# 120 further TensorE products of 128 to 512 columns behind the last product of a windowed-attention and gated-convolution kernel

## The chip, the cores and the metric

The kernel runs on one core of one Trainium2 chip. The metric is device time in microseconds of one execution. Times of the profile are microseconds from the start of the span, which goes from the first to the last instruction of the program on the core.

## The reference

Inputs are q, k and v of shape (8, 8, 576, 64) (batch, heads, positions, head width), a matrix w_in of 512 x 1024, three rows conv_w of 1024, and a matrix w_out of 1024 x 512. A causal attention with a window of 64 positions is followed by a layer with a gate, whose gate comes from a convolution along the positions:

```
scores = scale * np.matmul(q, k.transpose(0, 1, 3, 2))
mask = (rel >= 0) & (rel < window)
scores = np.where(mask, scores, -1000000000.0)
attn = np.exp(scores - max) / (sum + 1e-09)
x = np.matmul(attn, v)              # heads side by side: (8, 576, 512)
h = np.maximum(x @ w_in, 0.0)
conv_out[s] = sum over k of conv_w[k] * h[s + k - 1]
out = h * (1 / (1 + np.exp(-conv_out))) @ w_out
```

(The lines are shortened; the row maximum and the row sum are those of the softmax.)

## The kernel before, in words

The 8 x 576 = 4608 positions are cut into 12 units of 384 columns (`NU`, `NX`). For each unit the kernel makes the scores of six 64-wide blocks per head (`qk`, L371), the masked row maximum on VectorE (`row_max`, L378), the exponentials on ScalarE (`exps`, L388), the normalised rows (`normalise`, L399), their transposes (`transpose_pe`, L404, for the first two units; by VectorE and small transfers for the others), and the product with v (`values`, L522). The attention's result is split into a high and a low part, `xh` and `xl`, so that products in the rounded float32 kind give nearly full precision: each product of the layer is three, high times high, low times high and high times low. `mm1` (L542) multiplies by w_in, whose parts lie in `wih` and `wil`: per unit 8 slices of 128 hidden columns times 4 slices of the inner dimension times 3, each product with 128x128 weights and 384 columns. Then come the relu (L565), the convolution (`conv_mid` L571, `conv_side` L578), the sigmoid (L585), the gate (L590) and its split into `gh` and `gl` (L594, L598). `mm2` (L607) multiplies by w_out (`woh`, `wol`): again 8 x 4 x 3 products a unit, of 384 or 386 columns.

The eight PSUM banks of 512 columns are two `sc` (scores), two `acc` (`values` and `mm1` take turns) and four `po` (`mm2`, one per 128 output columns). At the end of a unit `po` is copied into `ot` by ScalarE (L647) and VectorE (L649), which lies in a tile named `T`, and SyncE issues a transfer to DRAM. In the last unit there is one transfer for each of the first three output slices (L651); the fourth is copied and sent in two halves (L643, L644).

The order of the work is a plan: every piece of work is a `Work` with a due time, an engine and a cost, `queued` simulates the engines with these costs and gives one list, and the last two lines of `attention_moe` issue the list in that order. Between pieces of the first 110 us it also puts products of a tile `spare` (`keep_busy`, L219: 112 columns, always the same 128x128 weights), whose results nobody reads. The program's closing part has the line number of the launch call, L778 (L783 in the changed kernel): each engine drains, SyncE waits for its transfers, and the engines meet at semaphores before they end. The program's opening part has L771.

Of the kernel before, what the change touches and what calls it, by code (L numbers as in the profile page):

```python
# [174 lines left out]
def attention_moe(ctx: ExitStack, tc: tile.TileContext, q, k, v, w_in, conv_w, w_out, out):  # L175
# [533 lines left out]
    with tc.manual_schedule():  # L709
        for x in queued(plan, keep_busy):  # L710
            x.do()


_INS = ['q', 'k', 'v', 'w_in', 'conv_w', 'w_out']

# [66 lines left out]
```

## Time and profile before

| | us |
|---|---|
| median of two runs | 518.82 |
| the two runs | 517.61, 520.02 |
| span of the profiled execution | 514.3 |
| TensorE busy in that span | 504.4 |
| last product of TensorE starts | 509.75 |

The profile is of one execution; for that execution it states its span alone. In a row of the timeline the first number is the start and the second the length of a merged group of instructions, then come engine, line, operation, output and inputs, the weights' size, the shape and the count. PE is the product on TensorE, PEld the load of its weights; a trailing q (SPq, PEldq) is the engine's own sequencer, which issues transfers and handles semaphores. A row of a line's view has min/median/max of the duration in ns and then the first and the last start in us. In the rows of windows the last three numbers are the granted TensorE clock, the busy share of the DMA engines and the GB/s.

### The profile page before, as it was taken

To read this page: it belongs to the slowest core of one execution; us is meant where nothing else is said; L and a number is where in the kernel's file an instruction comes from. 1 tells how busy PE (TensorE), PEld (TensorE's weight loads), DVE (VectorE), ACT (ScalarE), POOL (GpSimd) and SP (SyncE) were. 2 spreads that over 40 slices of the span, in tenths; PEclk is the share of its full clock that TensorE was granted. 3 is DMA by queue.
4 is the path that set the end of the run, shared out by engine and by line. 5 is a ranking of instruction groups with operands and counts; after the bars stand their busy time and mean duration, and the time that the engine had idled before them with its cause. 6 is when DMAs were issued, how large, how long until landed. Compare 5 with 4: busy or idle time off the path is not lost.

```text
span 514.3 us, 14601 instructions
## 1 busy us (share of the span) xinstructions
PE 504.4 (98%) x5710; PEld 487.0 (95%) x5710; DVE 367.0 (71%) x1088; ACT 380.0 (74%) x1013; POOL 91.2 (18%) x188
## 2 busy tenths in 40 slices
PE   8989998999999999999999999999999999999996
PEld 8878997999999999999999999999999999999996
DVE  4999998987855767666686967666766766645870
ACT  5989998889577888597687696786877866534640
POOL 7113332212020131020220221212202102000000
PEclk9999999999999999999999999999999999999999
DMA  8984963538225244444344343442541321100111
GB/s 302 357 318 142 322 213 111 175 83 324 74 63 176 82 141 144 124 142 148 112 154 149 104 141 115 146 146 71 187 157 46 106 67 46 62 1 0 63 63 62
DMA packets 29461, 69.96 MB, mean 136 GB/s; under 512 B 5712, under 2 KB 17616, under 8 KB 29392
## 3 DMA queue, kind: packets, MB, share of 16 engines
q1 hardware_dynamic: 29392, 69.03, 40.3%
q8 instruction: 45, 0.74, 0.6%
q14 instruction: 24, 0.20, 0.1%
HBM read 47.73 MB, written 9.47 MB: 111 GB/s over the span
## 4 chain that ended last, share of the span: by engine, by line
PE 89%; DVE 5%; ACT 2%; DMA 2%; issue 0%; SPq 0%; DVEq 0%; ACTq 0%
PE po L607 40%; PE acc L542 36%; PE acc L522 6%; PE sc L371 5%; DVE s L378 2%; PE acc L219 1%; DMA bits<-in_w_out_dram 1%; DVE T L262 1%; ACT T L256 1%; DMA q<-in_q_dram 1%; PE po L371 1%; DVE wil L280 1%; DVE s L399 1%; ACT ub L409 0%; DVE xl L529 0%
## 5 line engine op out<-in xcount | busy, mean ns | idle before, releaser
L607 PE MATMUL po<-gh,woh 128*128 128x386 f32 (+1 forms) x384 | 132.7, 346 | 0.0
L607 PE MATMUL po<-gh,wol 128*128 128x386 f32 (+1 forms) x384 | 130.0, 339 | 0.0
L542 PE MATMUL acc<-xh,wih 128*128 128x384 f32 x384 | 129.8, 338 | 0.1
L607 PE MATMUL po<-gl,woh 128*128 128x386 f32 (+1 forms) x384 | 129.7, 338 | 0.0
L542 PE MATMUL acc<-xh,wil 128*128 128x384 f32 x384 | 128.8, 335 | 0.0
L542 PE MATMUL acc<-xl,wih 128*128 128x384 f32 x384 | 128.7, 335 | 0.0
L578 DVE SCALAR_TENSOR_TENSOR c<-hbuf,cw,c 128x386 f32<-128x386 f32 (+1 forms) x192 | 111.6, 634 | 16.3 <-ACT c L571 16.1
L388 ACT ACTIVATE s<-s,nm 128x96 f32<-128x96 f32 (+2 forms) x288 | 105.1, 369 | 3.0 <-DVE nm L378 2.8
L399 POOL TENSOR_TENSOR s<-s,r 128x768 f32<-128x768 f32 x27 | 41.8, 1547 | 231.0 <-DVE r L394 180.4
L607 PEld LDWEIGHTS po<-gh,woh 128*128 128x128 f32 x384 | 72.2, 188 | 2.5
L542 PEld LDWEIGHTS acc<-xh,wih 128*128 128x128 f32 x384 | 72.2, 188 | 0.7 <-ACT hbuf L565 0.2
L607 PEld LDWEIGHTS po<-gl,woh 128*128 128x128 f32 x384 | 72.4, 189 | 0.0
L607 PEld LDWEIGHTS po<-gh,wol 128*128 128x128 f32 x384 | 72.3, 188 | 0.0
L542 PEld LDWEIGHTS acc<-xh,wil 128*128 128x128 f32 x384 | 72.2, 188 | 0.0
L542 PEld LDWEIGHTS acc<-xl,wih 128*128 128x128 f32 x384 | 72.1, 188 | 0.0
L571 ACT ACTIVATE c<-hbuf,cw 128x386 f32<-128x386 f32 (+1 forms) x96 | 53.6, 609 | 18.4 <-DVE gl L598 18.3
L598 DVE TENSOR_TENSOR gl<-c,gh 128x772 fp32r<-128x772 f32 (+1 forms) x48 | 47.3, 986 | 22.8 <-ACT gh L594 21.9
L590 DVE TENSOR_TENSOR c<-c,hbuf 128x772 f32<-128x772 f32 (+1 forms) x48 | 46.3, 972 | 19.9 <-ACT c L585 19.7
L378 DVE CUSTOM_DVE_ANT_0 s<-sc,mask 128x96 f32<-128x96 f32 (+2 forms) x260 | 49.1, 254 | 16.0 <-PE sc L371 15.5
L594 ACT CAST gh<-c 128x772 fp32r<-128x772 f32 (+1 forms) x48 | 40.1, 836 | 24.1 <-PE po L607 15.5
L388 ACT ACTIVATION_READ_ACCUMULATOR s<-s,nm 128x1 f32 x288 | 55.0, 191 | 0.0
L565 ACT ACTIVATE hbuf<-acc 128x384 f32<-128x384 f32 x64 | 30.9, 484 | 28.3 <-PE acc L542 28.3
(63 smaller groups left out, 561.1 us busy)
## 6 DMA issues: line engine op xcount, KB each, us to landing
v<-in_v_dram SPq DMA_DIRECT2D x24, 768.0 KB, 5.8
ub<-T SPq DMA_DIRECT2D x240, 48.0 KB, 1.9
k<-in_k_dram SPq DMA_DIRECT2D x22, 448.0 KB, 4.1
q<-in_q_dram SPq DMA_DIRECT2D x22, 384.0 KB, 5.6
out_dram<-T SPq DMA_DIRECT2D x8, 772.0 KB, 3.7
bits<-in_w_in_dram SPq DMA_DIRECT2D x8, 512.0 KB, 8.7
bits<-in_w_out_dram SPq DMA_DIRECT2D x8, 512.0 KB, 5.7
out_dram<-T SPq DMA_DIRECT2D x3, 768.0 KB, 4.8
```

The lines of the kernel that those rows point to most:

```text
L371: nc.tensor.matmul(bank_of(u, b, i, h)[r:r + rows, o:n], qs[hs, 2 * g + p, t:t + rows], ks[hs, 2 * g + p, t + o:t + n], start=True, stop=True)
L378: nc.vector.tensor_tensor_reduce(out=ss[b][:, i, h, o:n], in0=bank_of(u, b, i, h)[:, o:n], in1=mask[m][:, o:n], scale=-0.125, scalar=3.0e3 ...
L388: nc.scalar.activation(x, x, AF.Exp, bias=nms[b][:, e], scale=-1.0, accum_out=sms[b][:, e])
L399: on.tensor_tensor(sv, sv, rs[b][:, e].unsqueeze(2).broadcast_to([P, e.stop - e.start, n]), ALU.mult)
L542: nc.tensor.matmul(acc[bank(("m", u, f))][:, :NX], w[:, f, c], x[u % 2][:, c], start=(c == 0 and j == 0), stop=(c == NC - 1 and j == 2))
L565: nc.scalar.activation(hbuf[:, f, o:o + NX], ps[:, :NX], AF.Relu)
L571: nc.scalar.activation(cs[i % 2][:, a, :n], hbufs[u % 2][:, f, 1:1 + n], AF.Copy, scale=cw[:, 1, f:f + 1])
L578: nc.vector.scalar_tensor_tensor(c, hbufs[u % 2][:, f, e:e + n], cw[:, e, f:f + 1], c, op0=ALU.mult, op1=ALU.add)
L590: nc.vector.tensor_tensor(c, c, hbufs[u % 2][:, 2 * i:2 * i + 2, 1:1 + n], ALU.mult)
L594: nc.scalar.copy(ghs[ring(u, i)][:, :, :n], cs[i % 2][:, :, :n])
L598: nc.vector.tensor_tensor(gls[ring(u, i)][:, :, :n], cs[i % 2][:, :, :n], ghs[ring(u, i)][:, :, :n].bitcast(F32), ALU.subtract)
L607: nc.tensor.matmul(po[o][:, :n], w[:, f, es], x, start=(f == 0 and j == 0), stop=(f == NF - 1 and j == 2))
```

## The change

Behind the loop that issues the plan, still in the same program, ten groups of twelve products are issued on TensorE. Group g writes the first n columns of `acc[g % 2]`, each product with its own start and stop. The moving operand is always the first n columns of `xh[1]`, read across its four slices (4 x 384 columns lie side by side). The weights are the 128x128 blocks of `wih`, block number `i // reuse`: a new block for each product where `reuse` is 1, the same block for all twelve where it is 12, a new block for every second where it is 2. Nothing reads these results.

```
     for x in queued(plan, keep_busy):
         x.do()
 
+    flat_x, flat_w = xh[1].rearrange("p c n -> p (c n)"), wih.rearrange("p f c e -> p (f c) e")
+    for g, (n, reuse) in enumerate(((512, 1), (512, 12), (448, 1), (416, 1), (384, 1), (384, 12), (384, 2), (256, 1), (128, 1), (128, 12))):
+        for i in range(12):
+            nc.tensor.matmul(acc[g % 2][:, :n], flat_w[:, i // reuse], flat_x[:, :n], start=True, stop=True)
```

On TensorE the listings of the two programs differ in the last rows; `acc_107` and `acc_108` are the two `acc` banks, `xh_64` is `xh[1]`, and the shape is partitions x columns.

```order
@@ -1,3 +1,3 @@
-L778 UNCONDITIONAL_BRANCH
+L783 UNCONDITIONAL_BRANCH
 L219 MATMUL acc_107<-spare 128x112 x9
 L371 MATMUL sc_105<-k,q 64x64
@@ -3429,3 +3429,13 @@
 L607 MATMUL po_112<-gh_97,wol 128x386
 L607 MATMUL po_112<-gl_100,woh 128x386
-L778 UNCONDITIONAL_BRANCH
+L716 MATMUL acc_107<-xh_64,wih 128x512 x12
+L716 MATMUL acc_108<-xh_64,wih 128x512 x12
...
+L716 MATMUL acc_107<-xh_64,wih 128x128 x12
+L716 MATMUL acc_108<-xh_64,wih 128x128 x12
+L783 UNCONDITIONAL_BRANCH
```

All rows ahead of these, on TensorE and on the other engines, are the same in both programs but for the line numbers of the launch; the new products stand between the last L607 product and the closing part.

## The prediction

> **What bounds the kernel now.** I read the page first: its busy shares, its clock digits and its chain.
>
> ```profile
> span 514.3 us, 14601 instructions
> PE 504.4 (98%) x5710; PEld 487.0 (95%) x5710; DVE 367.0 (71%) x1088; ACT 380.0 (74%) x1013; POOL 91.2 (18%) x188
> PEclk9999999999999999999999999999999999999999
> PE 89%; DVE 5%; ACT 2%; DMA 2%; issue 0%; SPq 0%; DVEq 0%; ACTq 0%
> ```
>
> TensorE is busy for 98% of the span, holds 89% of the chain that ended last, and has its clock granted all the way. Work added to it in the middle would cost its full length. This work is added at the end, so what matters is what else still runs when TensorE is done. Next I read the chain of waits near its end and the timeline of the last two microseconds.
>
> ```profile
> 471.94 38.16 PE po L607 x216
> 510.10 0.02 issue
> 510.12 0.37 DVE T L643
> 510.49 0.02 issue
> 510.52 0.32 ACT T L643
> ...
> 509.75 0.34 PE L607 MATMUL po<-gl,woh 128*128 128x386 f32 x1
> 510.59 0.90 SPq L644 DMA_DIRECT2D out_dram<-T  x2
> ```
>
> The last 216 products of L607 run without a gap, 38.16 / 216 = 0.177 us each, and the last ends at 509.75 + 0.34 = 510.09. Two half copies by VectorE and ScalarE follow, then two transfers to DRAM, the second of which is issued by 511.5. The span ends at 514.3, so 4.2 us pass after the last product. The view of the end-of-program line L778, SyncE's waits there and the landing time of the last transfers tell what fills them.
>
> ```profile
> L778 SPq EVENT_SEMAPHORE  x7: 17/27/28, 513.0 to 514.2; - x7
> L778 POOLq EVENT_SEMAPHORE  x4: 17/17/17, 513.6 to 514.2; - x4
> L778 SPq DRAIN  x3: 7/7/7, 513.6 to 513.9; - x3
> L778 PEldq DRAIN  x2: 13/1695/3377, 506.8 to 513.9; - x2
> ...
> SPq L778 <- DMA out_dram<-T: 1.8, 2, 1.5
> ...
> L644 SPq DMA_DIRECT2D out_dram<-T x2: 402/406/409, 510.6 to 511.1; - x2
> ...
> DMA to landing us min/median/max: 2.2/2.3/2.4
> ```
>
> TensorE's sequencer reaches its drain at 506.8 and stands in it for 3.38 us, to about 510.15: it is finished 0.05 us after its last product. SyncE waits for the last transfer (issued at about 511.1, 2.2 us to landing, so 513.3), and the engines meet at 513.6, where GpSimd's first semaphore row stands. From that meeting to the end of the span it is 514.3 - 513.6 = 0.7 us. **TensorE therefore has 513.6 - 510.15 = 3.45 us of cover**: so much added work is free, and every microsecond beyond it moves the meeting and the end by one.
>
> **The change, part by part.** It removes nothing and moves nothing. It adds 120 products on TensorE behind the last L607 product: 24 of 512 columns, 12 of 448, 12 of 416, 36 of 384, 12 of 256 and 24 of 128, together 12288 + 5376 + 4992 + 13824 + 3072 + 3072 = 42624 columns. Their operands (xh, wih) were written long before, the banks (acc) were last read long before, and the listing of the changed program has no wait on them, so I let the first start right behind the last L607 product and the rest follow without a gap. No transfer, no copy and no other engine's instruction is added. The copies and transfers of the tail read other banks and buffers than these products write; were one late, it would have the added length itself as cover.
>
> The price of one product is its start-to-start time, not its record, since the records overlap. The nearest rows are those of L542: same weights, same kind of data, 384 columns, in a stretch where TensorE waits for nothing.
>
> ```profile
> L542 PE MATMUL acc<-xh,wil x31: 334/334/337, 61.1 to 76.7; 128*128 128x384 f32 x31
> L542 PEld LDWEIGHTS acc<-xl,wih x31: 187/188/188, 61.1 to 76.7; 128*128 128x128 f32 x31
> ...
> 16.01 1.39 PE L404 MATMUL po<-ident,s 128*128 128x128 f32 x11
> ...
> L404 PE MATMUL po<-ident,s x11: 272/273/295, 16.0 to 17.1; 128*128 128x128 f32 x11
> ...
> L219 PE MATMUL acc<-spare 128*128 128x112 f32 x74 | 12.2, 332 | 1.0 <-DVE spare L222 1.0
> L219 PEld LDWEIGHTS acc<-spare 128*128 128x128 f32 x74 | 11.3, 240 | 1.7 <-DVE spare L222 1.0 <-issue 0.7
> ```
>
> Of three interleaved groups, one has 31 products from 61.1 to 76.7, so 30 steps of three: 15.6 / 90 = 0.1733 us for 384 columns, 0.4514 ns a column. L607 with 386 columns took 0.177. The narrow end has only plain float32 rows: the 128-column transposes of L404 start (1.39 - 0.27) / 10 = 0.112 us apart, when the last record of 0.27 us is taken off.
>
> Widths other than these two have no row, so each is bounded from both sides:
> - By columns alone (all of the 173.3 ns streams): 512 columns 231.1 ns, 448 202.2, 416 187.8, 384 173.3, 256 115.6, 128 57.8. The sum is 42624 x 0.4514 = 19.24 us.
> - By a line through the two rows (0.24 ns a column and a fixed part of 81): 204, 189, 181, 173, 143 and 112 ns. The sum is 24 x 204 + 12 x 189 + 12 x 181 + 36 x 173.3 + 12 x 143 + 24 x 112 = 19.98 us.
> - By columns, but no product under 112 ns: 19.24 + 24 x (112 - 57.8) / 1000 = 20.54 us.
> - No product under the 173.3 of a 384-column one, if the weight load (a record of 188 ns, longer than the spacing) set that spacing: 19.24 + 24 x 0.1155 + 12 x 0.0577 = 22.7 us.
>
> These ends are close together, because wide products lose in the second reading what narrow ones gain. I take the first, 19.24, and raise it by 0.1, some 3 ns on each of the 36 narrow ones, since the 4 ns between L542 and L607 are not two columns: **19.35 us**. The rows of L542 are of the very operands used here. L404 and L219 work on other data (float32 instead of the rounded kind), and L219 has 18 records between 1 and 5 us for 9 calls in the program, so that kind is issued in another way than the products of L542, which are one to a call.
>
> [...]
>
> Repeated weights: in 36 products all twelve of a group have the same weights, and 12 more have each twice. I price them like the others. The L219 rows are that case: every product has the same 128x128 tile as its weights, and there are as many weight loads as products (x74 and x74). If the repeated load (11 + 11 + 11 + 6 = 39 of them) were nevertheless left out, the first reading, in which a load has no price, saves nothing; the second saves at most its fixed part, 39 x 0.081 = 3.2 us, so 16.8 us in all and a time of 532.2.
>
> The sum: TensorE's last product ends at 510.09 + 19.35 = 529.44, its drain 0.05 later, the end 0.7 later, at 530.2. Against 514.3 that is **+15.9 us** (19.35 - 3.45). The page gives no time of the profiled execution but its span of 514.3; the two timed runs lie 3.3 and 5.7 us above that, their median 518.82 lies 4.5 above. What lies around the span is launch and end, which the change does not touch, so I add to the median: 518.82 + 15.9 = **534.7 us**.
>
> **The rivals.**
>
> *Narrow products have a floor (slower than forecast).* The 128-column products cost 112 ns or more each, because a weight load cannot be finished sooner. For it: L404's spacing, and load records of 188 ns beside a spacing of 173. Against it: those rows are float32. With the 20.54 us of above the time is 518.82 + 17.1 = 535.9; with 22.7 it is 538.1.
>
> *More than two products in flight (not slower by over 2%).* A record of L542 lasts 334 ns and the next starts after 173, so about two are under way at once. Those products add up in one bank in a chain of twelve; the added ones stand alone, each with its own start and end. If that chain is what holds the spacing, three could be under way: 334 / 3 = 111 ns for 384 columns, 42624 x 0.290 = 12.4 us, +8.9, so 527.7. It decides if the spacing falls below (10.4 + 3.45) / 42624 = 0.325 ns a column, 10.4 us being 2% of 518.82. Against it: L607 changes bank after every three products and gains nothing by it (0.177). [...]
>
> *The change does not do what it says (same).* Products that nobody reads could be dropped, or run elsewhere. Against it: the listing has all 120 as the last rows before TensorE's last branch, and the L219 products, which nobody reads either, are in the trace. The time would be 518.8.
>
> *The clock falls (much slower).* At the start, under the throttle, 18 products of L219 take longer.
>
> ```profile
> 1.05 4.18 PE L219 MATMUL acc<-spare 128*128 128x112 f32 x18 [1.05 <-DVE spare L222]
> L219 PE MATMUL acc<-spare x18: 421/421/553, 1.0 to 4.8; 128*128 128x112 f32 x18
> ...
> 10.69 1.37 PE L219 MATMUL acc<-spare 128*128 128x112 f32 x10
> L219 PE MATMUL acc<-spare x10: 275/275/363, 10.7 to 11.8; 128*128 128x112 f32 x10
> ...
> 512.00:512.10 0.10, 0.00 (x0) 0.00 (x0) 0.00 (x0) 0.00 (x0) 0.00 (x0) 1.00 0.60 201
> 512.20:514.30 2.10, 0.00 (x0) 0.00 (x0) 0.00 (x0) 0.00 (x0) 0.00 (x0) 0.50 0.07 22
> ```
>
> Their spacing is (4.18 - 0.42) / 17 = 0.22 against (1.37 - 0.28) / 9 = 0.12, nearly double. The granted clock falls to 0.50 at 512.1, some 2 us after the last product. If the added work ran so, 19.35 would become 35 to 38 us and the time about 552. It needs a gap of about 2 us ahead of the added work, and I see none.
>
> **How the numbers follow.** My forecast, 534.7, gets 0.62. The floor for narrow products (535.9 to 538.1) gets 0.28, the falling clock (552) 0.04, three in flight (527.7) 0.03, no effect 0.02; 0.01 is kept for a gain by a cause that I don't see. Slower by over 2%, about what a measurement of this kernel can tell from no change, means over 529.2: 0.62 + 0.28 + 0.04 = 0.94. Within 2% are 0.03 + 0.02 = 0.05, and faster 0.01. The range ends below at 532.2, where repeated loads are left out in the second reading, and above at 538.1, the worst floor. The spread of the two runs (517.61 to 520.02, 1.2 to each side of their median) lies inside it around the forecast. The falling clock, three in flight and no effect lie outside.
>
> **What would show it.** In the profile of the changed kernel the span should be about 530.2, with 5830 products on TensorE and as many loads; the first L716 row should start near 509.93, 0.18 after the last L607 product; 12 products of 512 columns should take 2.7 to 2.8 us, 12 of 384 2.1 with new and with repeated weights alike, 12 of 256 1.4 to 1.5 and 12 of 128 0.7 to 0.8. SyncE's wait at the end should be for TensorE instead of for out_dram, and the clock should stay granted to the last product. 12 products of 128 columns in 1.35 us or more would give it to the floor. The prediction is wrong if the span grows by less than 13 or more than 20 us, if repeated weights take a visibly different time, or if the tail's copies and transfers move.

## The result and the profile after

The changed kernel took 533.47 us (median of 532.54 and 534.41) against 518.82 before, a ratio of 1.031 with a 95% interval of 1.027 to 1.035. It is 14.65 us slower by these medians. The forecast was 534.7, in a range of 532.2 to 538.1.

The first rows are from the page of the changed kernel, whose profiled execution is the one that took 534.41 us.

```profile
span 532.6 us, 14841 instructions
PE 524.5 (98%) x5830; PEld 504.6 (95%) x5830; DVE 367.4 (69%) x1088; ACT 380.1 (71%) x1013; POOL 87.5 (16%) x188
PEclk9999999999999999999999999999999999999999
```

TensorE has 120 products and 120 weight loads more, and its clock is granted to the end. What stands around this span is 534.41 - 532.6 = 1.8 us. The timeline of the changed kernel shows where the new products lie:

```profile
510.92 0.34 PE L607 MATMUL po<-gl,woh 128*128 128x386 f32 x1
511.10 20.63 PE L716 MATMUL acc<-xh,wih 128*128 128x512 f32 x120
511.77 0.90 SPq L644 DMA_DIRECT2D out_dram<-T  x2
```

The first starts 0.18 us after the start of the last L607 product, about the step from one L607 product to the next (0.177). They run without a gap for 20.63 us. The merged row has the name of the first shape, it stands for all 120. The last transfers are issued 0.85 us after the start of that L607 product, as before (509.75 and 510.59), so the tail's own work was not held up.

The closing part, in the view of its line and in SyncE's waits (changed kernel):

```profile
L783 SPq EVENT_SEMAPHORE  x7: 17/28/17112, 514.2 to 532.6; - x7
L783 POOLq EVENT_SEMAPHORE  x4: 17/17/17, 532.0 to 532.5; - x4
...
SPq L783 <- PE acc L716: 17.1, 1, 17.1
```

SyncE now stands 17.1 us in a wait for the last L716 product, where before its longest wait there was 1.5 us for a transfer. The end is TensorE's: its last product ends at 511.10 + 20.63 = 531.73, the engines meet at 532.0, and the span ends at 532.6, 0.9 us after that product. Before, 4.2 us passed there.

The widths can be told apart by cutting the stretch at the start of each group (view of windows, changed kernel; the first number after the bounds is the length, then TensorE's busy time with a count of the products that touch the window):

```profile
511.10:516.57 5.47, 5.47 (x25) 4.51 (x25) 0.36 (x1) 0.54 (x2) 0.00 (x0) 1.00 0.41 144
516.57:519.00 2.43, 2.43 (x13) 2.25 (x12) 0.00 (x0) 0.00 (x0) 0.00 (x0) 1.00 0.00 0
519.00:521.26 2.26, 2.26 (x13) 2.24 (x12) 0.00 (x0) 0.00 (x0) 0.00 (x0) 1.00 0.00 0
521.26:527.51 6.25, 6.25 (x37) 6.25 (x37) 0.00 (x0) 0.00 (x0) 0.00 (x0) 1.00 0.01 3
527.51:528.93 1.42, 1.42 (x13) 1.42 (x13) 0.00 (x0) 0.00 (x0) 0.00 (x0) 1.00 0.00 0
528.94:531.73 2.79, 2.79 (x26) 2.65 (x24) 0.00 (x0) 0.00 (x0) 0.00 (x0) 1.00 0.00 0
```

The products in these windows are 24 of 512 columns, 12 of 448, 12 of 416, 36 of 384, 12 of 256 and 24 of 128, so the spacings are 228, 203, 188, 174 and 119 ns (the last to the start of the next group at 528.94), and for 128 columns, with the last record of 0.28 us taken off, (2.79 - 0.28) / 23 = 109 ns. That is a mean: in the trace the first step behind the wider products is 61 ns, the others are 110 to 115. From 384 to 512 columns that is 0.42 ns a column; from 256 to 128 it is 0.08 ns. The narrow products have a floor, that is, a least spacing whatever their width. New weights, weights in pairs and one weight for all twelve make no difference in the 384-column stretch:

```profile
L716 PE MATMUL acc<-xh,wih x34: 334/334/334, 521.6 to 527.3; 128*128 128x384 f32 x34
L716 PEld LDWEIGHTS acc<-xh,wih x34: 187/188/188, 521.6 to 527.3; 128*128 128x128 f32 x34
```

These 34 of the 36 take (527.3 - 521.6) / 33 = 0.173 us each, with records of 334 ns throughout, and as many loads stand beside them.

### The profile page after: what moved, and what is told of

Same layout as the page of the kernel before. It is cut to its first block, busy times and chain, and to the rows that moved or that the text cites. A ratio compares the mean times of both kernels' runs of the same rounds, so it can differ in the third digit from the quotient of the medians.

```text
span 532.6 us, 14841 instructions
## 1 busy us (share of the span) xinstructions
PE 524.5 (98%) x5830; PEld 504.6 (95%) x5830; DVE 367.4 (69%) x1088; ACT 380.1 (71%) x1013; POOL 87.5 (16%) x188
## 4 chain that ended last, share of the span: by engine, by line
PE 80%; DMA 7%; ACT 6%; DVE 3%; SPq 2%; issue 1%; ACTq 0%; DVEq 0%
PE po L607 37%; PE acc L542 30%; PE acc L522 6%; PE sc L371 4%; PE acc L716 4%; DMA bits<-in_w_in_dram 3%; DMA bits<-in_w_out_dram 3%; ACT s L388 2%; ACT T L256 1%; SPq L437 1%; DVE s L378 1%; DMA q<-in_q_dram 1%; DVE T L262 1%; ACT L585 0%; ACT c L585 0%
## 5 line engine op out<-in xcount | busy, mean ns | idle before, releaser
L607 PE MATMUL po<-gh,woh 128*128 128x386 f32 (+1 forms) x384 | 132.7, 345 | 0.0
L607 PE MATMUL po<-gh,wol 128*128 128x386 f32 (+1 forms) x384 | 130.0, 339 | 0.0
L607 PE MATMUL po<-gl,woh 128*128 128x386 f32 (+1 forms) x384 | 129.6, 338 | 0.0
L578 DVE SCALAR_TENSOR_TENSOR c<-hbuf,cw,c 128x386 f32<-128x386 f32 (+1 forms) x192 | 111.5, 634 | 16.2 <-ACT c L571 15.9
L607 PEld LDWEIGHTS po<-gh,woh 128*128 128x128 f32 x384 | 72.2, 188 | 2.5
L607 PEld LDWEIGHTS po<-gl,woh 128*128 128x128 f32 x384 | 72.3, 188 | 0.0
L607 PEld LDWEIGHTS po<-gh,wol 128*128 128x128 f32 x384 | 72.2, 188 | 0.0
L378 DVE CUSTOM_DVE_ANT_0 s<-sc,mask 128x96 f32<-128x96 f32 (+2 forms) x260 | 49.1, 253 | 15.9 <-PE sc L371 15.8
```

Source lines behind the costliest of these rows:

```text
L378: nc.vector.tensor_tensor_reduce(out=ss[b][:, i, h, o:n], in0=bank_of(u, b, i, h)[:, o:n], in1=mask[m][:, o:n], scale=-0.125, scalar=3.0e3 ...
L578: nc.vector.scalar_tensor_tensor(c, hbufs[u % 2][:, f, e:e + n], cw[:, e, f:f + 1], c, op0=ALU.mult, op1=ALU.add)
L607: nc.tensor.matmul(po[o][:, :n], w[:, f, es], x, start=(f == 0 and j == 0), stop=(f == NF - 1 and j == 2))
```

## The experiments

**How large is the change?** From the start of the last L607 product to the end of the span, it is 514.3 - 509.75 = 4.6 us before and 532.6 - 510.92 = 21.7 after. That is 17.1 us, while the medians differed by 14.65. The same kernel was run again. The theory at this point: the added work takes 20.5 us, 3.3 us of it lie beside the last transfers, and the narrow products have a floor that the weight load sets.

> The changed kernel again, beside the kernel before, to settle the size. Theory one (what the trace of the first run shows): the end of the program grows by 21.7 - 4.6 = 17.1 us, counted from the start of the last L607 product to the end of the span, so the time grows by 17.1 us (3.3%); the 14.65 us between the first medians came from two runs of before that lie 2.4 us apart. Rival: the time grows by 14.7 us (2.8%), and some 2.5 us of the added products are hidden in a way that the trace of one execution does not show.

Measured: 534.66 us (5 runs) against 517.35 (17 runs, from 516.04 to 519.94), 17.3 us more, ratio 1.033 (1.031 to 1.036). The timeline of this run has the same tail:

```profile
511.72 0.34 PE L607 MATMUL po<-gl,woh 128*128 128x386 f32 x1
511.90 20.63 PE L716 MATMUL acc<-xh,wih 128*128 128x512 f32 x120
```

The span was 533.4, so it is 533.4 - 511.72 = 21.7 us once more. Theory one holds. The first medians rest on two runs each, and the kernel before spreads over 3.9 us; its first two runs had a median 1.5 us above that of the 17, and the first two of the changed kernel one 1.2 us below that of the 5. The spread lies ahead of the change: the last L607 product started at 509.75, 510.92 and 511.72 in the three profiles so far, with the same instructions in the same order ahead of it.

**The narrow groups left out.** The edit takes the last two entries of the table away:

```
-    for g, (n, reuse) in enumerate((..., (384, 2), (256, 1), (128, 1), (128, 12))):
+    for g, (n, reuse) in enumerate((..., (384, 2), (256, 1))):
```

> The change without its two groups of 128 columns (96 products). Theory one: a 128-column product costs 0.111 us, a floor, so the time is 24 x 0.111 = 2.7 us under that of the changed kernel and 14.5 us over before. Rival (cost by columns alone, 0.058 us each): 1.4 us under the changed kernel.

Measured: 532.48 us (6 runs), 2.2 us under the changed kernel and 15.1 over before, ratio 1.029 (1.026 to 1.032). The medians alone lie between the two expectations and do not tell them apart; the trace decides, since it is free of the spread ahead:

```profile
511.94 17.99 PE L716 MATMUL acc<-xh,wih 128*128 128x512 f32 x96
```

20.63 - 17.99 = 2.64 us went with 24 products, 110 ns each. By columns alone it would have been 1.4. Theory one holds.

**The first group alone.** Only the entry `(512, 1)` stays, 12 products.

> The first group of the change alone: 12 products of 512 columns, 2.7 us. Theory one: TensorE has 3.45 us between its last product and the meeting of the engines, so this costs nothing: within 0.3 us of before, and 4.6 us from the last L607 product to the end, as before. Rival (work at the end costs its length, because the tail's copies and transfers are slowed or because TensorE itself closes late): 2.7 us more than before.

Measured: 517.95 us (12 runs) against 517.35, ratio 1.001 (0.998 to 1.003): no difference. In the timeline, the view of L783 and SyncE's waits of this run:

```profile
512.63 0.34 PE L607 MATMUL po<-gl,woh 128*128 128x386 f32 x1
512.81 2.91 PE L716 MATMUL acc<-xh,wih 128*128 128x512 f32 x12
...
L783 POOLq EVENT_SEMAPHORE  x4: 17/17/17, 516.3 to 516.9; - x4
...
SPq L783 <- DMA out_dram<-T: 1.4, 1, 1.4
```

The 12 products follow the last L607 product and end at 512.81 + 2.91 = 515.72; the engines meet at 516.3, and SyncE's wait is for out_dram again, not for TensorE. From the last L607 start to the end it is 517.0 - 512.63 = 4.4 us, no more than the 4.6 of before. Theory one holds: 2.7 us of TensorE at this place are free.

**The same products, 24 products earlier.** The groups are issued ahead of the last eight pieces of TensorE's work (24 products of L607):

```
+    work = queued(plan, keep_busy)
+    last = [i for i, x in enumerate(work) if x.eng == "PE"][-8]
+    for j, x in enumerate(work):
+        if j == last:
...
+                    nc.tensor.matmul(acc[g % 2][:, :n], flat_w[:, i // reuse], flat_x[:, :n], start=True, stop=True)
         x.do()
```

> The same 120 products, put 24 products of L607 ahead of the end instead of behind it. Theory one: no cover there, so they cost their whole length, 20.5 us over before, 3.4 us more than the changed kernel. Rival (where they stand does not matter, the added length is the same): 17.1 us over before, as the changed kernel.

Measured: 538.25 us (6 runs), 20.9 over the median of before, ratio 1.041 (1.038 to 1.044), and 3.6 over the changed kernel. The end of its chain of waits:

```profile
507.68 20.44 PE acc L717 x120
528.12 4.29 PE po L607 x24
532.41 0.02 issue
532.43 0.37 DVE T L643
```

The 120 products take 20.44 us, as at the end, and by the medians the whole of it counts. So the end does hide about what was forecast: 3.3 us by the traces (4.2 us passed behind the last product before, 0.9 after the change), 3.6 by these medians.

**Where the floor sets in.** The table of the change is replaced by eight groups of other widths, with new weights each:

```
-    for g, (n, reuse) in enumerate(((512, 1), (512, 12), ...)):
+    for g, (n, reuse) in enumerate(((400, 1), (320, 1), (240, 1), (192, 1), (160, 1), (96, 1), (64, 1), (32, 1))):
```

> Instead of the ten groups, eight groups of twelve products with new weights each, of 400, 320, 240, 192, 160, 96, 64 and 32 columns. Theory one (13.3 ns and 0.417 ns a column, but never under the 111 ns that the load of 128 weight columns takes): 180, 147, 113, then 111 for each of the five narrow ones. Rival (13.3 ns and 0.417 ns a column all the way, and the 111 ns belong to the two groups of 128 as they stood): 180, 147, 113, 93, 80, 53, 40, 27.

This run and the three behind it were timed once each (525.88, 524.33, 524.72 and 517.91 us, in the order in which they stand here), so they are read by their traces alone. The windows of this run, cut at the start of each group, without the last group:

```profile
511.09:513.26 2.17, 2.17 (x14) 2.17 (x13) 0.36 (x1) 0.54 (x2) 0.00 (x0) 1.00 0.91 326
513.26:515.01 1.75, 1.75 (x13) 1.75 (x13) 0.00 (x0) 0.00 (x0) 0.00 (x0) 1.00 0.15 47
515.01:516.35 1.34, 1.34 (x14) 1.34 (x13) 0.00 (x0) 0.00 (x0) 0.00 (x0) 1.00 0.00 0
516.35:517.67 1.32, 1.32 (x14) 1.32 (x13) 0.00 (x0) 0.00 (x0) 0.00 (x0) 1.00 0.00 0
517.67:519.00 1.33, 1.33 (x15) 1.33 (x13) 0.00 (x0) 0.00 (x0) 0.00 (x0) 1.00 0.00 0
519.00:520.31 1.31, 1.31 (x15) 1.31 (x14) 0.00 (x0) 0.00 (x0) 0.00 (x0) 1.00 0.05 13
520.31:521.63 1.32, 1.32 (x14) 1.32 (x14) 0.00 (x0) 0.00 (x0) 0.00 (x0) 1.00 0.00 0
```

Divided by 12: 181 ns for 400 columns, 146 for 320, 112 for 240, and then 110, 111, 109 and 110 for 192, 160, 96 and 64. From 240 columns down the width costs nothing at all. Theory one holds, the rival fails. What sets the floor is open with this run: the load, or some least time between products.

**Fewer weight columns, and chains.** Five groups with 64 or 32 weight columns, then twelve full products in one chain in one bank, and twelve that change bank:

```
+    for g, (m, n) in enumerate(((64, 384), (64, 128), (32, 384), (32, 128), (32, 64))):
+        for i in range(12):
+            nc.tensor.matmul(acc[g % 2][:m, :n], flat_w[:, i, :m], flat_x[:, :n], start=True, stop=True)
+    for i in range(12):
+        nc.tensor.matmul(acc[1][:, :384], flat_w[:, i], flat_x[:, :384], start=i == 0, stop=i == 11)
+    for i in range(12):
+        nc.tensor.matmul(acc[i % 2][:, :384], flat_w[:, i], flat_x[:, :384], start=True, stop=True)
```

> Instead of the ten groups: twelve products each with 64 weight columns and 384 moving columns, 64 and 128, 32 and 384, 32 and 128, 32 and 64; then twelve of 384 columns with full weights summed up in one bank in one chain, and twelve that change bank each time. Theory one (the floor is the load of the weights, which goes by their columns): 173 ns at 384 whatever the weights; at 128 moving columns 64 weight columns lower the floor of 111 to some 56, so the 67 ns by width decide, and 32 weight columns give 67 too; 32 and 64 gives 40. Chain and changing banks: 173 each. Rival (a full-clock product of this kind cannot start more often than every 111 ns, whatever its weights): 111 for all of 64 and 128, 32 and 128, 32 and 64. Second rival (the chain sets the spacing): 173 in the chain, less with changing banks.

The windows of this run, by group, in this order:

```profile
511.25:513.33 2.08, 2.08 (x13) 1.61 (x12) 0.36 (x1) 0.54 (x2) 0.00 (x0) 1.00 0.93 332
513.33:514.05 0.72, 0.72 (x14) 0.71 (x12) 0.00 (x0) 0.00 (x0) 0.00 (x0) 1.00 0.42 138
514.05:516.12 2.07, 2.07 (x16) 1.29 (x14) 0.00 (x0) 0.00 (x0) 0.00 (x0) 1.00 0.00 0
516.12:516.84 0.72, 0.72 (x14) 0.72 (x12) 0.00 (x0) 0.00 (x0) 0.00 (x0) 1.00 0.00 0
516.84:517.22 0.38, 0.38 (x15) 0.38 (x13) 0.00 (x0) 0.00 (x0) 0.00 (x0) 1.00 0.00 0
517.22:519.41 2.19, 2.19 (x18) 2.19 (x15) 0.00 (x0) 0.00 (x0) 0.00 (x0) 1.00 0.03 7
519.41:521.65 2.24, 2.24 (x13) 1.92 (x12) 0.00 (x0) 0.00 (x0) 0.00 (x0) 1.00 0.00 0
```

With 384 moving columns it is 173 ns whatever the weights. With 128 moving columns it falls from 111 to 60 when the weights have 64 columns, and stays at 60 with 32; 32 and 64 gives 32. So there is no least time of 111 between products, and the first rival fails. The sizes by theory one (67, 67, 40) were 7 to 8 ns too high: of the fixed 13 ns beside the wide products some 7 are left at 128 columns (60 - 128 x 0.417). The chain took 182 ns each, with a slow start behind the narrow weights; with changing banks it is (2.24 - 0.34) / 11 = 173. A chain doesn't make the spacing, nor does a change of bank shorten it, so the second rival fails too.

**The load by its columns.** 32 moving columns, so that the stream is short, and 128, 96, 64 and 32 weight columns; then full weights with widths around the hand-over:

```
+    for g, (m, n) in enumerate(((128, 32), (96, 32), (64, 32), (32, 32), (128, 224), (128, 240), (128, 256), (128, 272))):
+        for i in range(12):
+            nc.tensor.matmul(acc[g % 2][:m, :n], flat_w[:, i, :m], flat_x[:, :n], start=True, stop=True)
```

> Instead of the ten groups: twelve products each of 32 moving columns with 128, 96, 64 and 32 weight columns, then with full weights 224, 240, 256 and 272 moving columns. Theory one (the load of the weights sets the floor, 111.6 ns for 128 columns, and goes by columns): 112, 84, 56 and 28 ns for the first four; 112, 112, 119 and 127 for the others, so that the floor hands over to the width between 240 and 256. Rival (the load has two sizes only, a full one of 112 ns and a fast one for fewer columns): 112, then some 25 to 30 for the other three.

The windows of this run, without the last group:

```profile
512.81:514.07 1.26, 1.26 (x14) 1.26 (x13) 0.36 (x1) 0.53 (x2) 0.00 (x0) 1.00 0.97 352
514.07:515.09 1.02, 1.02 (x15) 1.02 (x14) 0.00 (x0) 0.00 (x0) 0.00 (x0) 1.00 0.86 295
515.09:515.79 0.70, 0.70 (x15) 0.70 (x14) 0.00 (x0) 0.00 (x0) 0.00 (x0) 1.00 0.21 67
515.79:516.17 0.38, 0.38 (x16) 0.38 (x14) 0.00 (x0) 0.00 (x0) 0.00 (x0) 1.00 0.00 0
516.17:517.58 1.41, 1.41 (x17) 1.41 (x15) 0.00 (x0) 0.00 (x0) 0.00 (x0) 1.00 0.00 0
517.58:518.94 1.36, 1.36 (x15) 1.36 (x13) 0.00 (x0) 0.00 (x0) 0.00 (x0) 1.00 0.04 12
518.94:520.38 1.44, 1.44 (x14) 1.44 (x13) 0.00 (x0) 0.00 (x0) 0.00 (x0) 1.00 0.00 0
```

By twelfths it is 105 ns for 128 weight columns (in the trace its second product follows the first after 27 ns, the others come every 111 to 112), 85 for 96, 58 for 64 and 32 for 32: from 32 to 96 columns 53 ns, 0.83 ns a weight column and some 5 ns beside. The floor goes by the columns of the weights, in steps as theory one had them, and the rival with two sizes fails. The records of the loads go the same way (view of lines on the weight loads; the last number ahead of the second bar is the mean in ns):

```profile
L716 PEld LDWEIGHTS acc<-xh,wih 128*96 128x96 f32 x12 | 1.1, 165 | 0.0
L716 PEld LDWEIGHTS acc<-xh,wih 128*64 128x64 f32 x12 | 0.8, 138 | 0.0
L716 PEld LDWEIGHTS acc<-xh,wih 128*32 128x32 f32 x12 | 0.5, 113 | 0.0
```

From 32 to 96 weight columns the record of a load grows by 52 ns and the spacing by 53, so it is the load that sets the floor. At 256 moving columns the spacing is 120 ns: there the width takes over. At 240 it is 113, and at 272, in the group left out here, 125 by the trace. The 118 at 224, where 112 was expected, hold one step of 188 ns behind the narrow weights; the other steps of that group are 109 to 114.

**The same bytes as 2-byte numbers.** Three groups of 384, 128 and 64 columns with full weights, both operands read as bfloat16; the sums mean nothing and nobody reads them:

```
+    half_x, half_w = flat_x.bitcast(mybir.dt.bfloat16), flat_w.bitcast(mybir.dt.bfloat16)
+    for g, n in enumerate((384, 128, 64)):
+        for i in range(12):
+            nc.tensor.matmul(acc[g % 2][:, :n], half_w[:, i, :P], half_x[:, :n], start=True, stop=True)
```

> Instead of the ten groups: twelve products each of 384, 128 and 64 columns whose 128x128 weights and moving columns are the same bytes read as 2-byte numbers. Theory one (the floor of 111 ns is the time to read 128 weight columns of 4 bytes): the floor is half or less, so 173 ns at 384 or a little under, 56 to 67 at 128 and 40 to 56 at 64. Rival (the load goes by columns, not by bytes): 111 at 128 and at 64, as with 4 bytes.

The windows of this run, by group:

```profile
511.72:513.68 1.96, 1.96 (x13) 1.19 (x13) 0.36 (x1) 0.53 (x2) 0.00 (x0) 1.00 0.96 345
513.68:514.35 0.67, 0.67 (x14) 0.67 (x12) 0.00 (x0) 0.00 (x0) 0.00 (x0) 1.00 0.52 168
514.35:514.87 0.52, 0.52 (x15) 0.39 (x12) 0.00 (x0) 0.00 (x0) 0.00 (x0) 1.00 0.00 0
```

163 ns at 384, 56 at 128, and (0.52 - 0.19) / 11 = 30 at 64, when the last record of some 0.19 us is taken off (the load record of this kind is 98 ns). With 2-byte weights no floor shows down to 64 columns, although the weights have 128 columns, and the outputs 128 rows. The rival fails. Theory one was right that 2-byte weights have a lower floor, but its reason does not give the size: half the bytes would leave a floor of 56, and 30 was measured at 64. The load records give an estimate. Those of 32 and 96 weight columns (113 and 165 ns) are 0.81 ns a column and 87 fixed; taking 87 off leaves some 101 ns for 128 columns of 4 bytes (188) and some 11 for 128 of 2 bytes (98). Weights and moving columns were changed together here, so this run does not say whose kind matters.

## Why the prediction was right, and where it was off

*The bound and the place.* Right: nothing on TensorE hides the new work, the engines' meeting at the end waits for it, and the clock stays granted. That the tail is not disturbed held as well.

*The cover.* Right, with 3.3 us for the forecast's 3.45: behind the last product 4.2 us passed before and 0.9 after. The difference is in the closing part: SyncE itself waits for the last product and only then goes on, so the end comes 0.9 us after it, where the forecast had 0.05 + 0.7. The run with 12 products showed the cover free of cost, the run with the products earlier showed what it is worth.

*The price of the wide products.* Right: by columns 5.55, 2.43, 2.25, 6.24 and 1.39 us were reckoned for the groups from 512 to 256 columns, and 5.47, 2.43, 2.26, 6.25 and 1.42 were measured. But the reading behind it, that all of the 173.3 ns streams, does not hold: the slope is 0.42 ns a column with some 13 ns fixed. The errors, 3 ns too much at 512 columns and 3 too little at 256, are small and nearly cancel, since 384 columns lie between. The second reading, with 204 ns at 512 and 143 at 256, fails at both.

*The price of the narrow ones.* This is the step that failed: "no product under 112 ns" was the third reading, and the first was taken, with 57.8 ns and 3 added. The 24 products of 128 columns took 109 to 111 ns each, 2.6 us in all and not 1.4 to 1.5. The sign set for the floor, 1.35 us for twelve, was a hair too high to be met: 12 x 112 is 1.34. The two reasons given against the row of L404 (another kind of data, and issued otherwise) did not carry: its 112 ns hold for the rounded kind too. The rival of the narrow floor, with its 20.54 us, was the right one, though it had only 0.28; 20.5 us were measured. Its second form, 173 ns for every narrow product, is refuted. The load does not set the spacing of 384 columns, although its record of 188 ns is longer (173 ns with 32 weight columns too); it sets that of widths up to 240.

*Repeated weights.* Right: a repeated load costs as a new one.

*The sum.* +15.9 us were forecast against a median of 518.82. The cost is 17.1 by the trace and 17.3 by the larger set of runs, so the sum was 1.2 to 1.4 us too small, nearly all of it the narrow products. That the first medians show 14.65 comes from both pairs of runs: those of before lie 1.5 us above what 17 runs give, those after 1.2 below what 5 give. The forecast's closeness to 533.47 is thus partly luck: too small a cost, on too high a start. The 4.5 us between the span of before and the median are not launch and end, as the prediction had it. In the later runs 1.7 to 1.9 us stand around the span (one of before took 516.04, with a span of 514.3). So the profiled execution took an estimated 516.1, less than both timed runs, and the other 2.7 us are the spread between executions.

*The other rivals.* Three in flight would need under 0.325 ns a column; 0.44 was measured at 512. The products are all there, and the clock never fell while they ran. For the slow L219 products at the start the trace shows the spacing alone: the granted clock of that stretch is printed as 1.00 (windows from 1.0 to 5.0 us), so the throttle named there is not shown.

On the Trainium skill, page "TensorE: Matmul & The Clock Gate": the load by columns / 1.2 ("LDWEIGHTS (loading the stationary operand)") gives an estimate of 106.7 ns for 128 columns and 0.83 ns a column. The runs agree with the 0.83 ns a column, and their 112 ns at 128 are 5 more. The fast load ("Weight-path perf modes — Fast Weight Load (FWL) and DoubleRow") is on for 128 weights of a kind that is not FP32, and reads 32 bits at a time, with no win for fp32. The rounded float32 kind shows no fast load here (the floor of 111 ns); with 2-byte weights the trace agrees with one (30 ns at 64 columns). The sustained 131 ns at 512 ("Back-to-back issue gap") fail, with 228 measured.

What stays open: why products of 4-byte data with wide streams take some 10 ns more than 2-byte ones (173 and 163 at 384 columns) although the floor that their load sets is only 112; and why the executions differ by up to 3 us ahead of the last L607 product. One cause shows in the traces of the last two runs above: TensorE stood idle for 2.3 and 1.9 us ahead of 84.5 and 83.2 us, and then ran at a granted clock of 0.50 for 3.4 us. In the trace of before it stood idle for 1.6 us there and kept its clock, so the first three profiles do not differ by this.

## What to carry to other kernels

Price work on an engine by the start-to-start time of the nearest row, and ask of every row which of its two parts, stream or load, set that time: for full weights of rounded float32, fewer than some 240 moving columns are not cheaper here, so the width up to there is free to use. Work behind an engine's last instruction is free only as far as the closing part waits for something else, here 3.3 us for the last transfers. Where a cost can be read as the tail of one trace, measured from the last instruction that both kernels share, do so: that gave 17.1 us when the medians of two runs gave 14.65.

## What the runs showed of the hardware

- Products of rounded float32 data with 128x128 weights, issued in a row, follow each other every 109 to 112 ns on the average of a group, from 32 to 240 moving columns (105 in the group whose second product came after 27 ns); from 256 (120 ns) they go by width, 0.42 ns a column (174 ns at 384, 228 at 512).
- This floor goes by the weights' columns: 85 ns at 96, 58 at 64, 32 at 32, and the record of the load goes with it (165, 138 and 113 ns).
- The same weights twelve times in a row cost as much as new ones, 173 ns at 384 columns.
- 2-byte weights of 128 columns with 2-byte moving columns show no such floor: 56 ns at 128 moving columns and 30 at 64.
